# Partial sums of the second softmax on GpSimd in three batches, and another instruction order

## The chip, the cores and the metric

One core of one Trainium2 chip runs the kernel. The metric is the device time of one execution in microseconds; three runs of the kernel before are shown, and a hardware profile of one execution.

## The reference

There are 8 batches of 8 heads with 576 tokens of 64 features, and 32 packed queries `p` per head. Attention runs twice, and a token-mixing layer follows.

```python
def sm_attn(qq, kk, vv):                    # scale = 1/8
    s = scale * np.matmul(qq, kk.transpose(0, 1, 3, 2))
    s = s - np.max(s, axis=-1, keepdims=True)
    a = np.exp(s)
    a = a / (np.sum(a, axis=-1, keepdims=True) + 1e-09)
    return np.matmul(a, vv)
p_packed = sm_attn(p, k, v)                 # 32 rows per head
x = sm_attn(q, p_packed, p_packed)          # softmax over groups of 32
# x: (8, 576, 512) after the heads are put side by side
wq = x @ w_q;  wk = x @ w_k                 # 512 -> 64
W_tok = 0.125 * np.einsum('bsd,btd->bst', wq, wk)
mixed = np.einsum('bst,btd->bsd', W_tok, x)
out = np.maximum(mixed, 0.0) @ w_out
```

## The kernel before

Everything is written out as named operations, one closure each, and a string `SCHEDULE` says in which order they are issued. An item is `name@batch`, with the engine behind it where there is a choice (`v` VectorE, `s` ScalarE, `g` GpSimd, `p` SyncE), or the PSUM banks (`:31`) and a way to split a matmul into column halves (`c` all halves, `p` part, `f` none). Each engine works through its own queue in this order and waits on semaphores for what it needs. Nothing is reordered later: the string is the schedule.

The work of a batch, with the names that the text uses:

- `LK`, `LQ`, `LV` (line 153) load `k`, `q`, `v` of a batch through GpSimd's queue and cast to bf16 on the way; six buffers each. Batch 0 is loaded in halves (`LQA`, `LVB` and so on; `cA0` to `cB1` cast its `k`).
- `kt0` to `kt2` and `qt0` to `qt2` (line 262) transpose `k` and `q` on TensorE; `ke`, `qe` copy the result out of PSUM (`evict`, lines 141 to 149). For batch 0 the same steps are `kf`, `kfe`, `qf`, `qfe`.
- `s0` (321) computes the scores of the packed queries, `nm0` (335) their negative maximum on VectorE, `ex0`, `ex1` (344) the exponentials with their sums on ScalarE, `rc1` (360) the reciprocals.
- `xt0`, `xt1` (399) transpose the exponentials, `xe` copies them, `pv` (423) multiplies with `v`, `pp0`, `pp1` (439) scale the result, `pt` (453) transposes it, `pte` copies. In batch 0 these are done by halves: `xa`, `xb`, `xea`, `xeb`, `pvA`, `pvB`, `ptA`, `ptB`, `pteA`, `pteB`.
- `e0` (494, 507) computes the scores of the second attention: 128 rows with 36 groups of 32. `mx0` (523) takes the maximum of each group, `sb0` (526) subtracts it, `x0` (533) is the exponential on ScalarE in fp32, `sm0` (537, tile `rs`) sums each group, `rr0` (540) takes the reciprocal, `ml0` to `ml2` (561, tile `a`) multiply on GpSimd. Batch 0 does it in two parts (`mxA`, `mxB`, ...).
- `at`, `ae` transpose the normalised weights; `pq`, `pqe`, `wk`, `wke`, `wkx`, `wq`, `wqe`, `g`, `ge`, `y`, `ye` form the small factors of the mixing layer; `m0`, `m1`, `m2` (697, 719) apply them and `r00` to `r11`, `r2` are the evictions with ReLU.
- `o0` to `o4` (737) multiply with `w_out`, `oe0` to `oe4` evict, and `st0` to `st2` or `sc0` to `sc3` store.

`s0` and `e0` share one PSUM tile of three banks; the other results of TensorE go to five single banks. `wm` are matmuls without use ahead of and between the first steps.

The operation that the changed order begins to use is already defined, from line 549, but no item of the string before names it:

```python
def sm(b):
    src = S_[b].get("e4", S_[b].get("e3", S_[b]["e2"]))
    nc.vector.tensor_reduce(tile("rs", [P, NU, 1], fp32, b)[:, r], src[:, r], axis=AX, op=ADD)
...
def sp1(b):
    e = S_[b]["e2"]
    nc.gpsimd.tensor_tensor(tile("e3", [P, NU, L // 2], fp32, b), e[:, :, 0:L // 2], e[:, :, L // 2:L], op=ADD)
```

`NU` is 36 and `L` is 32, so `sp1` writes 36 groups of 16, and `sm` reads them where they exist.

Of the kernel before, what the change touches and what calls it, by code (L numbers as in the profile page):

```python
# [7 lines left out]


SCHEDULE = """  # L10
    wm@8:4 LP@0 LQA@0 LVA@0 cA0@0s cA1@0v LQB@0 wm@1:4 pc@0v kf1@0:2 LVB@0 tp@0:0 kf0@0:4
# [11 lines left out]
    pt@1:0c xe0@2v pte@1s m1@0:23 xe1@2v e0@1:c r10@0s LK@6 rc1@2 r11@0v kt1@3:4 mx0@1
    kt0@3:0 ke1@3s kt2@3:1 LK@5 ke2@3s pq@1:4 sb0@1 o1@0:3c pqe@1s LQ@4 o2@0:4c ke0@3v x0@1
    oe1@0v s0@3 oe2@0s o0@0:3c sm0@1 qt0@2:4 oe0@0s qt1@2:0 rr0@1 qt2@2:1 qe1@2s nm0@3
    o3@0:3c ml0@1g qe0@2s ml2@1g oe3@0v at0@1:2f ex1@3 ml1@1g pv@2:40 ae0@1v ex0@3 qe2@2v
    LV@4 at1@1:2c pp0@2 xt0@3:1f ae1@1s pp1@2 LQ@5 xt1@3:3f rc1@3 xe0@3v pt@2:0c wk@1:2c
    pte@2s e0@2:f wkx@1 LK@7 wke@1s kt0@4:4 xe1@3s mx0@2 g@1:1c wq@1:0 ge@1s y@1:2 wqe@1s
# [7 lines left out]
    qt2@4:4 pv@4:13 qe2@4s rr0@3 nm0@5 ml0@3g pq@3:4 g@2:0c pqe@3s LQ@7 pp1@4 ge@2s qt1@4:4
    ex1@5 pp0@4 y@2:3 ml1@3g ke1@6v pt@4:1f ye@2s at0@3:0f qe1@4v pte@4s m0@2:32 ex0@5
    ae0@3v ml2@3g m1@2:14 r00@2v LV@6 qt1@5:0 r01@2s e0@4:p qe1@5v LV@7 r10@2s xt1@5:3f
    mx0@4 at1@3:0f xt0@5:1f ae1@3s o1@2:2f xe1@5s sb0@4 qt0@5:0 xe0@5s wq@3:3 oe1@2s o0@2:1c
# [2 lines left out]
    rr0@4 qe2@5s s0@7 pp1@5 ml0@4g pp0@5 oe3@2s y@3:0 xt1@6:2f nm0@7 pt@5:1f xe1@6s ml2@4g
    xt0@6:4f at0@4:3f ml1@4g ye@3s o2@2:2f ae0@4v ex1@7 pte@5v at1@4:0f xe0@6v oe2@2s
    m2@3:1f ae1@4v qt0@6:4 ex0@7 rc1@6 st1@2 pq@4:3 qt2@6:0 qe0@6v qt0@7:2 pqe@4s st1@1
    qe2@6v e0@5:c r2@3s st0@2 qe0@7s wk@4:0f mx0@5 st0@1 xt0@7:4c wke@4s m1@3:23 o4@3:1f
    r11@3s wkx@4 r10@3s sb0@5 g@4:3f pv@6:02 ge@4s oe4@3s xe0@7v qt1@6:1 pp1@6 y@4:4 wq@4:3
    pp0@6 qe1@6s qt2@7:2 ye@4v xt1@7:0c x0@5 qe2@7v pt@6:4c o2@3:1f pte@6v xe1@7v wqe@4s
    sm0@5 o3@3:4f oe2@3s qt1@7:0 oe3@3s e0@6:p rr0@5 qe1@7v ml0@5g st1@3 m0@4:41 rc1@7 mx0@6
    pv@7:23 r01@4s ml2@5g r00@4s m0@3:10 ml1@5g pp1@7 o1@4:4c r01@3s pp0@7 r00@3s sb0@6
    pq@5:0 at0@5:2c pqe@5s at1@5:3c ae0@5s pt@7:1c o0@3:0c ae1@5v x0@6 pte@7v wk@5:2p  # L50
    o1@3:3c wkx@5 oe1@4s sm0@6 wke@5s m1@4:41 oe1@3s e0@7:p r11@4s wq@5:3 rr0@6 oe0@3s mx0@7
    g@5:2c ml0@6g r10@4s o0@4:1c st0@3 ge@5s wqe@5s st2@3 y@5:2 ml2@6g o3@4:0c sb0@7 ml1@6g
    ye@5s oe0@4s pq@6:2 at0@6:3c oe3@4s m2@5:4c pqe@6v st0@4 at1@6:1c x0@7 ae0@6v m0@5:20
    ae1@6v o2@4:3c r00@5v r2@5s sm0@7 wk@6:1p r01@5s o4@5:2c oe2@4s wq@6:0 wke@6v st1@4
    oe4@5s wkx@6 m1@5:43 rr0@7 g@6:1c st2@5 r10@5s r11@5v o0@5:2c ml2@7g ge@6s wqe@6v ml1@7g
    o3@5:1c oe0@5v ml0@7g at1@7:0c y@6:4 pq@7:3 o2@5:2c ye@6s pqe@7v oe3@5s ae1@7v at0@7:4c
    m0@6:31 ae0@7s o1@5:0c r00@6v oe2@5s r01@6v wk@7:3p st1@5 oe1@5s m1@6:24 wkx@7 o0@6:1c
    r10@6v st0@5 wke@7s r11@6s g@7:3c oe0@6s o1@6:2c ge@7v y@7:3 wq@7:0 oe1@6s o2@6:1c ye@7s
# [770 lines left out]
```

## Time and profile before

| what | value |
|---|---|
| median of 3 runs (121.89 to 122.12) | 122.09 us |
| profiled execution | 122.1 us |
| its span, first to last instruction | 120.3 us |
| granted TensorE clock | 0.996 |
| TensorE busy | 109.1 us (91%), 2121 matmuls |
| VectorE busy | 99.4 us (83%), 176 instructions |
| ScalarE busy | 86.8 us (72%), 169 instructions |
| GpSimd busy | 44.7 us (37%), 70 instructions |
| loads through GpSimd's queue | 14.49 MB, 72.2% of 16 DMA engines' span |

Busy times are unions over the span, and the engines overlap. The difference between the profiled execution and its span, 1.8 us, lies before the first and behind the last instruction. The end of a matmul is modelled, so that a TensorE shown as busy can still be one that streams with small gaps. Two instructions of VectorE or ScalarE in a row overlap by some 0.08 to 0.1 us in the timeline, so that the step from start to start is a little shorter than the duration in the row.

### The profile page before, as it was taken

The numbers are of one execution on the slowest core, as the hardware profiler recorded it, in microseconds if no ns is written. First come the engines' busy times: TensorE is split into PE (matmuls) and PEld (weight loads), VectorE is DVE, ScalarE is ACT, GpSimd is POOL, SyncE is SP. The second block draws the span as 40 slices with busy tenths as digits, with TensorE's granted clock in tenths as the row PEclk, the third lists the DMA queues.
The fourth block names the chain that finished last, engine by engine and source line by source line (L and its number), as shares of the span: only waits on it lengthen the run. The fifth ranks groups of instructions, "written<-read, shape, count | busy, mean of one in ns | idle before, by whom it ended". The sixth has DMA issues, their size and how long they took to land.

```text
span 120.3 us, 4812 instructions
## 1 busy us (share of the span) xinstructions
PE 109.1 (91%) x2121; PEld 76.5 (64%) x2121; DVE 99.4 (83%) x176; ACT 86.8 (72%) x169; POOL 44.7 (37%) x70
## 2 busy tenths in 40 slices
PE   5999786588999999999999999999999999999950
...
DVE  3278799968999979999999999989998999566330
ACT  4228634688568869996988999996889995665530
...
GB/s 70 375 165 195 207 208 190 207 208 206 211 205 212 204 209 208 206 208 207 208 226 306 290 209 208 209 255 398 225 180 1 106 335 197 70 230 267 185 291 171
DMA packets 18165, 25.47 MB, mean 212 GB/s; under 512 B 2272, under 2 KB 14816, under 8 KB 18144
## 3 DMA queue, kind: packets, MB, share of 16 engines
q0 software_dynamic: 13952, 14.49, 72.2%
...
q10 hardware_dynamic: 288, 0.39, 0.9%
q8 instruction: 16, 0.26, 0.8%
q14 instruction: 5, 0.04, 0.1%
...
## 4 chain that ended last, share of the span: by engine, by line
PE 70%; DVE 19%; POOL 2%; ACT 2%; issue 2%; POOLq 0%; DVEq 0%
PE o_ps L737 24%; PE tp_h L262 9%; PE warm L787 6%; PE pv L423 4%; PE m_ps L697 4%; PE tp_a L582 3%; DVE rs L537 3%; PE e_ps L507 3%; PE wq_ps L642 3%; PE tp_x L399 2%; POOL a L561 2%; PE s L321 2%; DVE e L526 2%; DVE mx L523 2%; PE wk_ps L619 2%
## 5 line engine op out<-in xcount | busy, mean ns | idle before, releaser
L561 POOL TENSOR_TENSOR a<-e,rr 128x512 bf16<-128x512 f32 (+1 forms) x24 | 19.3, 828 | 50.4 <-DVE rr L540 45.1
L737 PE MATMUL o_ps<-w_out,reluT 128*64 128x512 bf16 (+2 forms) x236 | 32.3, 373 | 0.1
L737 PEld LDWEIGHTS <-reluT 128*64 128x64 bf16 (+1 forms) x236 | 13.8, 108 | 9.6 <-issue 1.0
L143 ACT ACTIVATE o_sb<-o_ps 128x512 f32<-128x512 f32 x25 | 14.9, 602 | 3.7 <-PE o_ps L737 3.2
L143 ACT ACTIVATE kT<-tp_h 128x768 bf16<-128x768 bf16 (+2 forms) x13 | 9.8, 794 | 5.7 <-PE tp_h L262 5.6
L143 ACT ACTIVATE reluT<-m_ps 128x512 bf16<-128x512 f32 x20 | 11.5, 600 | 2.5 <-PE m_ps L697 2.2
L344 ACT ACTIVATE e1T<-s,nmax 128x576 bf16<-128x576 f32 x16 | 11.8, 755 | 0.6 <-DVE nmax L338 0.5
L262 PE MATMUL tp_h<-ident,q_sb 128*64 128x128 bf16 x288 | 11.9, 221 | 0.2 <-ACT pqk L143 0.2
L533 ACT ACTIVATE e<-e 128x1152 f32<-128x1152 f32 (+2 forms) x9 | 9.5, 1059 | 3.3 <-DVE e L526 3.3
L262 PEld LDWEIGHTS <-q_sb 128*64 128x64 bf16 x288 | 9.8, 110 | 2.8 <-issue 1.7
L523 DVE TENSOR_REDUCE mx<-e_ps 128x36 f32<-128x1152 f32 (+2 forms) x9 | 10.9, 1208 | 0.7 <-PE e_ps L507 0.4
L262 PE MATMUL tp_h<-ident,k_sb 128*64 128x128 bf16 x288 | 11.3, 226 | 0.0
L526 DVE TENSOR_TENSOR e<-e_ps,mx 128x1152 f32<-128x1152 f32 (+2 forms) x9 | 11.0, 1221 | 0.3
L537 DVE TENSOR_REDUCE rs<-e 128x36 f32<-128x1152 f32 (+2 forms) x9 | 10.9, 1211 | 0.2 <-ACT e L533 0.2
L262 PEld LDWEIGHTS <-k_sb 128*64 128x64 bf16 x288 | 9.7, 114 | 1.0 <-issue 0.2
L787 PE MATMUL warm<-ident 128*64 128x512 bf16 x44 | 8.4, 488 | 1.5 <-POOL ident masks.py:199 1.4
L335 DVE TENSOR_REDUCE nmax<-s 128x2 f32<-128x1152 f32 x7 | 9.3, 1327 | 0.0
L145 DVE TENSOR_SCALAR reluT<-m_ps 128x512 bf16<-128x512 f32 x12 | 8.1, 679 | 1.3 <-PE m_ps L697 1.3
L149 DVE COPY qT<-tp_h 128x768 bf16<-128x768 bf16 (+2 forms) x16 | 8.4, 533 | 0.8 <-PE tp_h L262 0.4
L423 PE MATMUL pv<-v_sb,e 64*128 64x256 bf16 x126 | 8.1, 270 | 0.0
L582 PE MATMUL tp_a<-ident,a 128*64 128x128 bf16 (+1 forms) x113 | 6.4, 221 | 1.7 <-POOL a L561 1.7
L143 ACT ACTIVATE qT<-tp_h 128x768 bf16<-128x768 bf16 (+1 forms) x9 | 7.1, 798 | 0.9 <-PE tp_h L262 0.7
...
## 6 DMA issues: line engine op xcount, KB each, us to landing
...
k_sb<-in_k_dram POOLq DMA_DIRECT2D x7, 576.0 KB, 14.3
q_sb<-in_q_dram POOLq DMA_DIRECT2D x7, 576.0 KB, 18.3
v_sb<-in_v_dram POOLq DMA_DIRECT2D x7, 576.0 KB, 16.4
k_f<-in_k_dram SPq DMA_DIRECT2D x2, 576.0 KB, 4.3
...
```

What stands on the lines that cost most here:

```text
L143: nc.scalar.activation(dst, src, func, scale=scale)
L262: nc.tensor.transpose(dst[64 * g2:64 * g2 + 64], src[:, g2], ident)
L344: nc.scalar.activation(tile("e1T", [P, NJ, 2, 64], bf16, b)[:, :, h2], S_[b]["s1"][0][h2].rearrange("r (j s) -> r j s", j=NJ), EXP, bias=S ...
L423: nc.tensor.matmul(ps[h2], S_[b]["e1"][r, j, :], S_[b]["v_sb"][r, :, j, :].rearrange("s (g gp) d -> s gp g d", gp=2), start=(j == 0), stop ...
L523: nc.vector.tensor_reduce(tile("mx", [P, NU, 1], fp32, b)[:, r], S_[b]["e"][:, r], axis=AX, op=MAX)
L526: nc.vector.tensor_tensor(tile("e2", [P, NU, L], fp32, b)[:, r], S_[b]["e"][:, r], S_[b]["mx"][:, r].to_broadcast((P, nu, L)), op=SUB,)
L533: nc.scalar.activation(e, e, EXP, scale=scale)
L537: nc.vector.tensor_reduce(tile("rs", [P, NU, 1], fp32, b)[:, r], src[:, r], axis=AX, op=ADD)
L561: (nc.gpsimd if on == "g" else nc.vector).tensor_tensor(tile("a2", [P, NU, L], bf16, b)[:, r], S_[b]["e2"][:, r], S_[b]["rr"][:, r].to_bro ...
L582: nc.tensor.transpose(tp[r, k - k0], a2(b, k % 4 if k < 8 else 4, k // 4)[:, r], ident)
L737: nc.tensor.matmul(ps[r], src[:, i, o:o + P][:, r], w_out[:, i, cols], start=(i == 0), stop=(i == 3),)
L787: nc.tensor.matmul(ps[r], ident[:, r], moving, start=True, stop=True)
```

## The change

Only `SCHEDULE` changes. Three items are new, `sp1@2`, `sp1@3` and `sp1@4`: in these batches GpSimd adds the first and the second 16 of each group of 32 exponentials, and `sm0` sums 16 per group. Batches 0, 1, 5, 6, 7 sum 32 as before. All other items are the same operations in another order: 38 evictions go from `v` to `s` and 34 from `s` to `v`, eight projections (five of them of batch 7) go from `c` to `f` and one from `f` to `c`, banks are assigned anew, and the 22 pairs of `wm` are spread differently. The string has one line more, so lines of the changed kernel are higher by one. The lines with batch 0's softmax, with the new items and with the end:

```diff
 SCHEDULE = """
...
-    wm@1:3 xa0@0:3 nmB@0 xa1@0:0 xea0@0s qf0@0:2 rcA@0 xea1@0v ex1@0 qf1@0:1 cw1@0 qfe0@0v
-    pvA@0:0 qfe1@0s xb0@0:4 pp0@0 xb1@0:2 xeb0@0s LQ@1 rcB@0 xeb1@0v ptA@0:1f qf3@0:3
-    pteA@0s qfe3@0v e0A@0 wm@4:1 mxA@0 sbA@0 pvB@0:0 LV@1 qf2@0:2 xA@0 pp1@0 qfe2@0v
+    xa1@0:2 rcA@0 sB@0 xea0@0v xea1@0s qf1@0:3 nmB@0 cw2@0 pvA@0:4 qfe1@0s qf0@0:0 ex1@0
+    pp0@0 wm@1:1 qfe0@0v ptA@0:1c LQ@1 rcB@0 xb1@0:3 pteA@0v xb0@0:0 e0A@0 xeb0@0v wm@2:4
+    xeb1@0v mxA@0 qf2@0:2 qfe2@0s pvB@0:4 sbA@0 pp1@0 qf3@0:2 xA@0 qfe3@0v ptB@0:3f smA@0
...
-    kt1@2:0 ke2@2s ml1@0g pq@0:2 ke1@2v pqe@0s wo0@0 ex1@1 at1@0:1c ae1@0v wo1@0 ex0@1
-    ke0@2v wq@0:1 LQ@2 wk@0:2p wqe@0s LV@2 s0@2 wkx@0 qt0@1:4 wke@0s LK@4 nm0@2 xt0@1:3f
+    kt1@2:3 ml1@0g pq@0:0 ex0@1 pqe@0v wo1@0 at1@0:1c ke1@2v ex1@1 wo0@0 ae1@0v ke2@2v
+    wk@0:3p LQ@2 wq@0:0 wkx@0 LV@2 s0@2 rc1@1 wke@0v wqe@0s xt1@1:4f LK@4 nm0@2 xt0@1:2f
...
-    r01@1v s0@4 x0@2 pp0@3 o0@1:3c pp1@3 nm0@4 r2@1s qt2@3:2 pq@2:0 qt0@3:4 qe2@3s o1@1:1c
-    qe0@3v pqe@2s sm0@2 oe0@1s o4@1:2c oe1@1s qt1@3:0 ex1@4 pt@3:3c qe1@3v kt2@6:1 ex0@4
+    o0@1:4c nm0@4 x0@2 qt1@3:1 o1@1:3c oe0@1s pp1@3 sp1@2 ex1@4 qe1@3v qt0@3:0 pp0@3 qt2@3:1
+    oe1@1s LQ@5 sm0@2 pq@2:4 o4@1:2c qe0@3s qe2@3v pqe@2s pt@3:3c ex0@4 kt2@6:1 pte@3v
...
-    ke2@5s o2@1:4f ae1@2v ae0@2s xt1@4:0f rc1@4 oe4@1s oe2@1v kt0@5:3 x0@3 wk@2:1p ke0@5v
-    st2@1 qt0@4:4 xe1@4v s0@5 wkx@2 qe0@4s st0@0 sm0@3 wq@2:0 wke@2s kt1@6:2 st1@0 wqe@2s
+    ke2@5s o2@1:4c ae0@2v ae1@2s rc1@4 oe4@1v kt0@5:1 x0@3 wk@2:0c ke0@5v st2@1 xt1@4:3f
+    wke@2v s0@5 oe2@1s wkx@2 sp1@3 qt0@4:1 xe1@4s st0@0 nm0@5 wq@2:2 qe0@4s st1@0 g@2:0c
+    qt2@4:4 wqe@2s sm0@3 pv@4:31 qe2@4s ge@2v rr0@3 ex0@5 kt1@6:2 pp1@4 ml0@3g pq@3:0 pp0@4
...
-    rc1@5 r11@2v wqe@3s qe0@5v wk@3:2p x0@4 s0@6 wkx@3 wke@3v kt0@7:4 oe0@2s nm0@6 kt2@7:3
-    kt1@7:0 ke0@7s qt2@5:2 g@3:1f ke2@7s ke1@7v o3@2:4f sm0@4 ex1@6 pv@5:30 ex0@6 ge@3v
+    oe1@2s xe0@5v wk@3:4p x0@4 o0@2:3c wkx@3 nm0@6 qt0@5:1 wke@3s kt0@7:2 sp1@4 oe0@2s
+    kt1@7:4 ke0@7s kt2@7:0 ke1@7v g@3:3f LV@6 ex1@6 sm0@4 o3@2:2f LV@7 ex0@6 ge@3v rr0@4
+    pv@5:43 qe0@5v ke2@7s ml1@4g oe3@2s s0@7 pp1@5 ml2@4g pp0@5 ml0@4g y@3:0 qt2@5:1 nm0@7
...
-    r00@7v r01@7s st1@6 o3@7:1c oe4@7s o1@7:2c st2@7 oe3@7v o0@7:0c oe1@7s sc3@7p o2b@7:3c
-    sc1@7p oe0@7s o2a@7:2c oe2b@7v sc0@7s oe2a@7v sc2b@7s sc2a@7p
+    o3@6:3f r00@7v r01@7s m2@7:1f oe3@6s o0@7:0f r2@7v st1@6 o2a@7:3f oe0@7s o3@7:1f oe2a@7s
+    sc0@7p sc2a@7s o4@7:2f oe3@7s o1@7:4f sc3@7p oe4@7s o2b@7:1f st2@7 oe1@7s oe2b@7v sc1@7s
+    sc2b@7p
 """
```

More of the change, by code (lines that the diff above doesn't have):

```diff
@@ L10 @@
 SCHEDULE = """
-    wm@8:4 LP@0 LQA@0 LVA@0 cA0@0s cA1@0v LQB@0 wm@1:4 pc@0v kf1@0:2 LVB@0 tp@0:0 kf0@0:4
-    lp@0v LK@1 wm@3:3 kfe0@0s kfe1@0v wm@2:3 cB1@0v LK@2 cB0@0v sA@0 wm@1:3 cw3@0 nmA@0
-    kf3@0:1 kf2@0:3 kfe3@0s cw0@0 tr@0:42 kfe2@0v ex0@0 wm@2:3 lq1@0v lq0@0s sB@0 cw2@0
-    wm@1:3 xa0@0:3 nmB@0 xa1@0:0 xea0@0s qf0@0:2 rcA@0 xea1@0v ex1@0 qf1@0:1 cw1@0 qfe0@0v
-    pvA@0:0 qfe1@0s xb0@0:4 pp0@0 xb1@0:2 xeb0@0s LQ@1 rcB@0 xeb1@0v ptA@0:1f qf3@0:3
-    pteA@0s qfe3@0v e0A@0 wm@4:1 mxA@0 sbA@0 pvB@0:0 LV@1 qf2@0:2 xA@0 pp1@0 qfe2@0v
@@ L17 @@
-    ptB@0:4c smA@0 pteB@0s e0B@0 rrA@0 mxB@0 ml0@0g kt2@1:3 kt1@1:1 sbB@0 ke2@1s kt0@1:0
-    LK@3 at0@0:4c ke0@1v xB@0 ke1@1v ae0@0s smB@0 s0@1 kt0@2:4 rrB@0 nm0@1 kt2@2:1 ml2@0g
-    kt1@2:0 ke2@2s ml1@0g pq@0:2 ke1@2v pqe@0s wo0@0 ex1@1 at1@0:1c ae1@0v wo1@0 ex0@1
-    ke0@2v wq@0:1 LQ@2 wk@0:2p wqe@0s LV@2 s0@2 wkx@0 qt0@1:4 wke@0s LK@4 nm0@2 xt0@1:3f
-    g@0:1f LV@3 qt1@1:0 ge@0s xe0@1s y@0:2 qe1@1v xt1@1:1c ye@0s rc1@1 xe1@1v ex0@2 m0@0:30
-    pv@1:21 r00@0v LQ@3 ex1@2 qe0@1v r01@0s qt2@1:3 pp1@1 xt0@2:4c pp0@1 xt1@2:1c qe2@1v
@@ L23 @@
[L23 to L28, printed above, removed]
@@ L29 @@
-    kt1@4:3 ye@1v kt2@4:1 ke0@4v ke1@4s pv@3:02 sb0@2 LV@5 ke2@4s m0@1:43 m2@1:1c r00@1s
-    r01@1v s0@4 x0@2 pp0@3 o0@1:3c pp1@3 nm0@4 r2@1s qt2@3:2 pq@2:0 qt0@3:4 qe2@3s o1@1:1c
-    qe0@3v pqe@2s sm0@2 oe0@1s o4@1:2c oe1@1s qt1@3:0 ex1@4 pt@3:3c qe1@3v kt2@6:1 ex0@4
-    pte@3v m1@1:40 rr0@2 kt0@6:3 r10@1s r11@1v e0@3:c ml1@2g ke2@6s ke0@6v o3@1:0f mx0@3
-    ml2@2g ml0@2g xt0@4:3f oe3@1s kt1@5:4 xe0@4v kt2@5:0 LQ@6 ke1@5s sb0@3 at1@2:3f at0@2:1f
-    ke2@5s o2@1:4f ae1@2v ae0@2s xt1@4:0f rc1@4 oe4@1s oe2@1v kt0@5:3 x0@3 wk@2:1p ke0@5v
@@ L35 @@
-    st2@1 qt0@4:4 xe1@4v s0@5 wkx@2 qe0@4s st0@0 sm0@3 wq@2:0 wke@2s kt1@6:2 st1@0 wqe@2s
[L36 to L39, printed above, removed]
-    rc1@5 r11@2v wqe@3s qe0@5v wk@3:2p x0@4 s0@6 wkx@3 wke@3v kt0@7:4 oe0@2s nm0@6 kt2@7:3
@@ L41 @@
-    kt1@7:0 ke0@7s qt2@5:2 g@3:1f ke2@7s ke1@7v o3@2:4f sm0@4 ex1@6 pv@5:30 ex0@6 ge@3v
[L42 to L58, printed above, removed]
@@ L59 @@
-    wqe@7v st0@6 m2@7:4c oe2@6v m1@7:02 o3@6:3c r11@7s r2@7v r10@7s m0@7:42 oe3@6s o4@7:0c
-    r00@7v r01@7s st1@6 o3@7:1c oe4@7s o1@7:2c st2@7 oe3@7v o0@7:0c oe1@7s sc3@7p o2b@7:3c
-    sc1@7p oe0@7s o2a@7:2c oe2b@7v sc0@7s oe2a@7v sc2b@7s sc2a@7p
+    wm@8:2 LP@0 LQA@0 LVA@0 cA0@0v LQB@0 wm@2:2 pc@0s cA1@0s wm@1:0 LVB@0 kf0@0:0 tp@0:4
+    LK@1 kf1@0:1 kfe0@0s lp@0v wm@1:2 wm@3:2 kfe1@0v LK@2 cB1@0s cB0@0v sA@0 cw3@0 kf3@0:2
+    nmA@0 kf2@0:0 tr@0:31 cw1@0 kfe3@0v ex0@0 kfe2@0v wm@4:4 lq1@0v lq0@0s cw0@0 xa0@0:0
@@ new lines @@
+    xa1@0:2 rcA@0 sB@0 xea0@0v xea1@0s qf1@0:3 nmB@0 cw2@0 pvA@0:4 qfe1@0s qf0@0:0 ex1@0
+    pp0@0 wm@1:1 qfe0@0v ptA@0:1c LQ@1 rcB@0 xb1@0:3 pteA@0v xb0@0:0 e0A@0 xeb0@0v wm@2:4
+    xeb1@0v mxA@0 qf2@0:2 qfe2@0s pvB@0:4 sbA@0 pp1@0 qf3@0:2 xA@0 qfe3@0v ptB@0:3f smA@0
+    pteB@0s e0B@0 rrA@0 mxB@0 ml0@0g kt2@1:3 kt1@1:4 sbB@0 ke2@1s kt0@1:1 LV@1 at0@0:2c
+    ke1@1v xB@0 LK@3 ke0@1v ae0@0s smB@0 s0@1 kt0@2:0 rrB@0 nm0@1 kt2@2:4 ke0@2s ml2@0g
+    kt1@2:3 ml1@0g pq@0:0 ex0@1 pqe@0v wo1@0 at1@0:1c ke1@2v ex1@1 wo0@0 ae1@0v ke2@2v
@@ new lines @@
+    wk@0:3p LQ@2 wq@0:0 wkx@0 LV@2 s0@2 rc1@1 wke@0v wqe@0s xt1@1:4f LK@4 nm0@2 xt0@1:2f
+    xe1@1s g@0:1f LV@3 qt0@1:3 ge@0s xe0@1s y@0:1 qe0@1v qt1@1:4 qt2@1:0 ye@0s qe1@1v ex1@2
+    m0@0:31 pv@1:42 r01@0v ex0@2 LQ@3 r00@0s xt0@2:1c pp0@1 qe2@1s pp1@1 m1@0:43 pt@1:2c
+    r11@0v pte@1s xe0@2s e0@1:c LK@6 r10@0s pq@1:2 mx0@1 kt1@3:3 pqe@1s kt2@3:1 LK@5
+    xt1@2:4c ke2@3s kt0@3:0 sb0@1 ke1@3s o2@0:2c o1@0:1c ke0@3v x0@1 oe2@0v s0@3 xe1@2s
+    o0@0:2c sm0@1 oe1@0s qt1@2:4 oe0@0s qt0@2:0 rr0@1 o3@0:3c nm0@3 qe0@2s ml0@1g qt2@2:1
@@ new lines @@
+    qe1@2s ml1@1g rc1@2 oe3@0v at0@1:2c ex0@3 pv@2:04 ae0@1v ex1@3 ml2@1g qe2@2v LQ@4
+    at1@1:3c pp1@2 xt1@3:2f ae1@1s pp0@2 LV@4 xt0@3:1f xe1@3v pt@2:4c wk@1:2c pte@2s xe0@3s
+    e0@2:f wke@1v wkx@1 wq@1:0 mx0@2 g@1:2c kt0@4:4 ge@1s wqe@1s y@1:2 kt1@4:3 rc1@3 ye@1v
+    kt2@4:1 ke1@4s ke0@4v pv@3:20 sb0@2 ke2@4s m0@1:43 m2@1:1c r00@1s r01@1v s0@4 r2@1s
+    o0@1:4c nm0@4 x0@2 qt1@3:1 o1@1:3c oe0@1s pp1@3 sp1@2 ex1@4 qe1@3v qt0@3:0 pp0@3 qt2@3:1
+    oe1@1s LQ@5 sm0@2 pq@2:4 o4@1:2c qe0@3s qe2@3v pqe@2s pt@3:3c ex0@4 kt2@6:1 pte@3v
@@ new lines @@
+    m1@1:04 rr0@2 kt0@6:3 r10@1v r11@1s ml2@2g e0@3:c ke2@6s ml0@2g o3@1:0f mx0@3 ke0@6s
+    ml1@2g xt0@4:1f oe3@1s kt1@5:4 xe0@4v LK@7 kt2@5:0 ke1@5s sb0@3 at0@2:1f LV@5 at1@2:3f
+    ke2@5s o2@1:4c ae0@2v ae1@2s rc1@4 oe4@1v kt0@5:1 x0@3 wk@2:0c ke0@5v st2@1 xt1@4:3f
+    wke@2v s0@5 oe2@1s wkx@2 sp1@3 qt0@4:1 xe1@4s st0@0 nm0@5 wq@2:2 qe0@4s st1@0 g@2:0c
+    qt2@4:4 wqe@2s sm0@3 pv@4:31 qe2@4s ge@2v rr0@3 ex0@5 kt1@6:2 pp1@4 ml0@3g pq@3:0 pp0@4
+    y@2:4 qt1@4:1 pqe@3s ye@2v ex1@5 pt@4:0f qe1@4v LQ@6 at0@3:4f pte@4v m0@2:31 ml1@3g
```

19 lines of the change are left out of this document (added).

## The prediction

> **What bounds the kernel now.** I began with the busy tenths and the DMA row of the page. TensorE and VectorE alternate between 9 and less until the twelfth slice, then both read 9 almost throughout; the loads move a steady 205 to 210 GB/s up to slice 20.
>
> ```profile
> PE   5999786588999999999999999999999999999950
> DVE  3278799968999979999999999989998999566330
> ACT  4228634688568869996988999996889995665530
> GB/s 70 375 165 195 207 208 190 207 208 206 211 205 212 204 209 208 206 208 207 208 226 306 290 209 208 209 255 398 225 180 1 106 335 197 70 230 267 185 291 171
> ```
>
> Then the busy times by stage, cut where TensorE starts `pv` of batches 2, 5 and 7 (40.3, 72.75, 87.4 us) and where it stops (116.1).
>
> ```profile
> 0.00:40.30 40.30, 33.73 (x662) 24.26 (x662) 32.32 (x63) 23.89 (x48) 23.23 (x44) 1.00 1.16 204
> 40.30:72.75 32.45, 32.19 (x688) 24.35 (x688) 31.03 (x52) 28.87 (x56) 11.85 (x15) 1.00 1.19 226
> 72.75:87.40 14.65, 14.58 (x288) 10.49 (x289) 13.86 (x28) 12.27 (x26) 2.70 (x4) 1.00 1.03 258
> 87.40:116.10 28.70, 28.63 (x492) 17.38 (x486) 21.75 (x36) 21.75 (x42) 6.94 (x9) 1.00 0.49 179
> ```
>
> The third busy column is VectorE: 31.03 of 32.45 in the second stage, so VectorE and TensorE are both full there. The last stage is TensorE's alone (28.63 of 28.70; VectorE 21.75). The chain of waits leaves TensorE once in the middle, at 57.8 us, for VectorE's queue:
>
> ```profile
> 59.41 0.33 DVE wkx L632
> 59.74 1.27 DVE rs L537
> 61.04 0.38 DVE rr L540
> 61.41 1.21 DVE nmax L335
> 62.63 0.79 DVE pp L439 x2
> ```
>
> So a shorter `rs` (op `sm0`) lies on the path. Last, when the loads land. The issue of `LV@5` starts at 44.16 and takes 27.1 us, so it lands at 71.3; `pv@5`, which needs it, starts at 72.75. Likewise `LQ@7` lands at 77.0 (use 77.7), `LV@6` at 79.8 (81.5), `LV@7` at 84.2 (87.4). TensorE never waits for a load, but here it runs only 0.7 to 3.2 us behind them.
>
> ```profile
> v_sb<-in_v_dram POOLq DMA_DIRECT2D x1, 576.0 KB, 27.1
> ```
> ```profile
> 72.75 1.16 PE L423 MATMUL pv<-v_sb,e 64*128 64x256 bf16 x18
> ```
>
> The prices come from the groups by shape:
>
> ```profile
> L561 POOL TENSOR_TENSOR a<-e,rr 128x512 bf16<-128x512 f32 x16 | 16.7, 1044 | 44.6 <-DVE rr L540 39.3 <-ACT qT L143 5.3
> L561 POOL TENSOR_TENSOR a<-e,rr 128x128 bf16<-128x128 f32 x8 | 3.2, 395 | 5.8 <-DVE rr L540 5.8
> L537 DVE TENSOR_REDUCE rs<-e 128x36 f32<-128x1152 f32 x7 | 9.4, 1344 | 0.2 <-ACT e L533 0.2
> L537 DVE TENSOR_REDUCE rs<-e 128x20 f32<-128x640 f32 x1 | 0.8, 809 | 0.0
> L537 DVE TENSOR_REDUCE rs<-e 128x16 f32<-128x512 f32 x1 | 0.7, 685 | 0.0
> ```
>
> **The change part by part.** *Sums on VectorE.* From 685 ns at 512 and 809 at 640 elements, 576 take 0.75 us in place of 1.34: 3 x 0.6 = -1.8 us, all in the two middle stages.
>
> *Adds on GpSimd.* From 395 ns at 128 and 1044 at 512, a multiply costs 1.69 ns an element; 576 would be 1.15 us. Bounds: 1.04 (the 512 row) and, since an fp32 result and two full inputs are not in the trace, twice 1.04, 2.1. I take 1.15, the nearest kind. Three cost 3.5 us on an engine busy for 11.85 of 32.45 us, hence nothing by themselves. The new wait is `x0` to `sp1` to `sm0`. Between `x0@2` and `sm0@2` VectorE's order holds `pp1@3`, `qe1@3`, `pp0@3` (1.25 us), so the cover is bare; ahead of `sm0@3` and `sm0@4` lie some 2 us (`nm0` among them). At 2.1 us the three waits come to about 2 us. Queued behind `sm0` are `rr0` and the evictions `pte@3`, `ge@2`, `pp@4`, `pp@5`, for which `e0` of the next batch waits. On GpSimd, `LQ@5` stands behind `sp1@2`, `LK@7` and `LV@5` behind the three multiplies of batch 2, `LV@6` and `LV@7` behind `sp1@4`. The loads keep their order, and their transfers, one after another at 2.8 us each, start at 58.3, 61.1, 65, 77 and 80 us; the issues move to about 50, 54, 55, 69 and 70, still 6 us ahead: nothing.
>
> *Evictions that change engine.* 38 go from VectorE to ScalarE and 34 the other way. With the steps from start to start in the timeline (VectorE: a 768-column copy 0.47, a 512 one from fp32 PSUM 0.60, 256 columns 0.34; ScalarE 0.70, 0.48, 0.28) VectorE loses 17.2 and gains 14.6 us, -2.6; ScalarE gains 4.8. With the sums, VectorE's steps up to `pv@2`, from there to `pv@5`, to `pv@7` and to the end were 29.6, 31.1, 14.1, 20.0 and become 28.5, 29.0, 14.0, 19.0; ScalarE's were 21.0, 27.2, 11.3, 19.6 and become 23.2, 28.0, 12.3, 20.4. TensorE has the same columns and the same 22 warm-up pairs.
>
> *First stage.* VectorE's -1.1, and more: it idles 0.45 before `ae1@0` and 0.70 before `wkx@0`. There the new order has `pqe@0`, `ke1@2` and `ke2@2`, and `wk@0` (0.45) before `wq@0` (0.62), so `wkx@0` comes sooner. Walking the queues with these steps from the landing of k: `nmB` stays at 11.5, but one eviction of `xea` is now ScalarE's and the other lies ahead of `nmB`, so `pp0@0` starts at 12.25, not 13.37; `mxA` at 14.25, not 15.21; `mx0@1` at 31.65, not 33.09; `pv@2` at 38.7, not 40.3. Between -1.1 (the work alone) and -2.2 (work and both idle times) I take the walk's -1.6. `LV@2` landed at 38.1, so it fits.
>
> *Middle.* VectorE's -2.1 to `pv@5` would bring that to 72.75 - 1.6 - 2.1 = 69.0; the walk, with its waits, gives 70.1. But `LV@5` lands at 71.3: the bytes ahead of it in the queues are the same (three stores, `st2@1`, `st0@0`, `st1@0`, stay before it). TensorE waits there until 71.35: the gain is cut to -1.4, with 1.2 to 2.3 us of spare that hide other losses up to that point. From `pv@5` to `pv@7` VectorE's work is unchanged. The stores of batch 2 come 1.1 us sooner and will share the engines with `LV@6`; `LV@7` took 4.4 us with them and 2.8 without, so up to 0.6 is lost, I take 0.2.
>
> *End.* From `pv@7` TensorE is the limit with the same work. Eight projections go undivided: 28 matmuls of 128 columns took 7.0 us, 1.0 per projection, and 192 of 64 took 24.3, 1.01 per projection: nothing. The last evictions and stores swap names and keep their number after the last matmul: 4.2 us as before, give or take 0.1.
>
> Sum: -1.4 + 0.2 = -1.2. The profiled execution took 122.1 us (span 120.3, 1.8 around it), as much as the median of 122.09; so **120.9**. This case reaches from 120.2 (nothing lost to the stores, 0.1 at the end, and 0.4 if part of the three stores, for which `LV@5` took 6.3 us after `LK@7` instead of 2.8, slips behind it) to 121.5 (adds at 2.1 us, 0.6 lost to the stores).
>
> [...] GpSimd ran its 24 multiplies beside a full VectorE at 389 to 395 and 1038 to 1060 ns, and the copies of VectorE beside those of batch 2 (53.5 to 55.9 us) took 0.54 and 0.48, as elsewhere. [...]
>
> **The rivals.** *Blocked VectorE, 0.04.* [...]
>
> *Loads do not limit, 0.07.* If `LV@5` to `LV@7` land sooner, VectorE's -3.4 up to `pv@7` comes through in part, about -2.5: 119.6. Against it: the loads run without a gap to 84 us.
>
> *Nothing left, 0.13.* In the second stage VectorE and ScalarE now stand at 29.0 and 28.0 beside TensorE's 29; three equally full in-order queues wait for each other more. If that eats 1.2 us beyond the spare, it is 122.1.
>
> *ScalarE late, 0.26.* It takes 4.8 us more. In the second stage it is busy for 28.87 and idle for 3.58. If those idle times are waits that stay, and the 0.9 us is added, the stage is 33.3; if the first stage also gains nothing, as ScalarE has 2.2 us more there, `pv@5` starts at 40.3 + 33.3 = 73.6 instead of 72.75, and the end is 123.0. It decides once the walk's 70.1 slips by over 2.65 us. For it: a ScalarE step that is late holds a PSUM bank and so TensorE. Against: its longest waits in that stage are 0.6 to 0.8 us.
>
> **How the numbers follow.** The forecast has 0.50. About 0.2% (0.24 us) is what a measurement can tell. Faster: 0.50 + 0.07 and 0.05 from "nothing left" and "blocked", 0.62; same: 0.09 from those two; slower: 0.26 + 0.03 = 0.29. The range goes from the low end of the forecast's case to the middle of "ScalarE late" and leaves out the 0.07 below and half of the 0.26 above: 120.2 to 123.0.
>
> **What would show it.** Right: three 576-element adds of about 1.15 us; `rs` at 0.75 three times; `mxA` near 14.3 and `pv@2` near 38.7; TensorE waiting for `LV@5` until about 71.3; `pv@7` to the last matmul 28.5. Wrong: `pv@5` after 72.5 with ScalarE's evictions ending TensorE's waits; adds over 2 us; `LV@5` landing elsewhere; TensorE idle after 88 us.

## The result and the profile after

The changed kernel takes 123.21 us (median of 11 runs, 122.47 to 124.09), the kernel before beside it 121.98 us (11 runs, 121.4 to 122.32): a ratio of 1.0102, with a 95% interval of 1.0074 to 1.013. It is slower, and lies above the range of the prediction too. The profiled execution took 122.64 us (span 120.9), so it lies at the low end of its runs.

The rows of the page of the changed kernel that answer to those of before:

```profile
PE   5999975699899999999989999999999999999900
...
DVE  3198899998699799979999988899999995776010
ACT  4267256769789869989989998999799995556610
...
GB/s 72 366 183 200 208 208 188 207 208 206 209 206 211 205 209 208 207 209 207 208 263 321 239 208 207 208 297 395 148 0 5 240 353 190 87 264 221 350 249 59
```

VectorE now reads 7 and 8 in more slices of the middle, ScalarE 9 more often, and TensorE reads 0 in the last two slices, where before it read 5 in the second last. Then the busy times by stage, cut where the changed kernel starts `pv` of batches 2, 5 and 7 and where TensorE stops (length, TensorE, its weight loads, VectorE, ScalarE, GpSimd):

```profile
0.00:39.26 39.26, 33.27 (x664) 23.22 (x664) 31.69 (x61) 26.09 (x50) 22.36 (x42) 1.00 1.15 206
39.26:71.66 32.40, 31.74 (x677) 23.71 (x677) 29.98 (x54) 29.42 (x55) 16.40 (x20) 1.00 1.19 226
71.66:86.44 14.78, 14.48 (x296) 10.86 (x299) 13.35 (x25) 13.68 (x27) 3.65 (x5) 1.00 1.07 264
86.44:115.04 28.60, 28.39 (x450) 16.71 (x446) 20.62 (x34) 22.05 (x43) 6.42 (x9) 1.00 0.49 183
```

Beside the stages of before (40.30, 32.45, 14.65, 28.70) the first is 1.04 us shorter, and the others are 0.05 shorter, 0.13 longer and 0.10 shorter: TensorE stops at 115.04 instead of 116.07. But the span then goes on for 5.8 us (120.86 - 115.04) where it was 4.3 (120.33 - 116.07). So in this execution the body won 1.0 us and the end lost 1.6.

What happens in the end shows in the DMA view of the last microseconds, in slices of 0.1 us from 117 to 121, first of the kernel before and then of the changed one:

```profile
GB/s 471 389 348 369 328 389 410 430 369 328 328 328 369 328 348 328 338 175 21 0 0 0 0 0 0 0 0 0 0 0 0 0 0 0 0 0 0 0 0 0
```
```profile
GB/s 123 164 164 287 451 348 389 348 379 389 338 389 226 164 0 0 0 20 10 10 10 10 10 10 0 0 0 0 0 0 0 0 0 0 0 0 0 0 0 0
...
q14 instruction: 1, 0.01, 0.5%
```

Before, the stores stop all at once at 118.8. After, fifteen of the sixteen engines have sent their data by 118.4; for 0.3 us no packet starts at all, and then a single engine trickles 1 KB packets, one in 0.1 us (10 GB/s), until 119.4. Queue 14, which carries instructions, has one packet in this window, of 8 KB, from 118.40 to 118.71. The last store (issued at 115.89) reports done from fifteen engines within 2.89 us and from the sixteenth after 3.95. The issues on SyncE's queue (start, length, line, tiles, how many), first of the kernel before and then of the changed one, show what is new: the store of `sc3`, both of `st2` and `sc2b` stand one behind the other:

```profile
113.27 1.15 SPq L754 DMA_DIRECT2D out_dram<-ox  x2
114.66 2.45 SPq L764 DMA_DIRECT2D out_dram<-o_sb  x3
```
```profile
112.24 2.27 SPq L765 DMA_DIRECT2D out_dram<-o_sb  x2
114.61 1.19 SPq L755 DMA_DIRECT2D out_dram<-ox  x2
115.89 0.57 SPq L765 DMA_DIRECT2D out_dram<-o_sb  x1
```

The last begins 0.85 us behind the last matmul; before, it was 0.49, and ScalarE's queue sent another at the same time. The groups by shape, for the new and the changed steps:

```profile
L553 POOL TENSOR_TENSOR e<-e 128x576 f32<-128x576 f32 x3 | 4.3, 1422 | 12.6 <-ACT e L534 12.6
...
L538 DVE TENSOR_REDUCE rs<-e 128x36 f32<-128x576 f32 x3 | 2.2, 747 | 0.1
```

### The profile page after: what moved, and what is told of

It is laid out like the page before. It is cut to its first block, busy times and chain, and to the rows that moved or that the text cites. A ratio compares the mean times of both kernels' runs of the same rounds, so it can differ in the third digit from the quotient of the medians.

```text
span 120.9 us, 4729 instructions
## 1 busy us (share of the span) xinstructions
PE 107.9 (89%) x2073; PEld 74.5 (62%) x2081; DVE 96.1 (79%) x172; ACT 91.4 (76%) x173; POOL 48.8 (40%) x73
## 4 chain that ended last, share of the span: by engine, by line
PE 52%; DVE 16%; DMA 9%; issue 8%; ACT 5%; POOL 5%; SPq 1%; POOLq 0%; ACTq 0%
PE o_ps L738 16%; PE tp_h L263 7%; DMA out_dram<-o_sb 5%; DMA k_f<-in_k_dram 4%; PE m_ps L698 4%; PE pv L424 4%; PE tp_a L583 3%; DVE rs L538 3%; PE s L322 3%; PE e_ps L508 2%; DVE e L527 2%; DVE mx L524 2%; PE wq_ps L643 2%; PE tp_x L400 2%; POOL a L562 2%
## 5 line engine op out<-in xcount | busy, mean ns | idle before, releaser
L738 PEld LDWEIGHTS <-reluT 128*64 128x64 bf16 (+1 forms) x208 | 13.1, 107 | 9.7 <-issue 0.8
L144 ACT ACTIVATE o_sb<-o_ps 128x512 f32<-128x512 f32 (+1 forms) x25 | 14.7, 595 | 2.3 <-PE o_ps L738 1.6
L144 ACT ACTIVATE reluT<-m_ps 128x512 bf16<-128x512 f32 x22 | 12.8, 604 | 2.1 <-PE m_ps L698 1.9
L144 ACT ACTIVATE qT<-tp_h 128x768 bf16<-128x768 bf16 (+2 forms) x14 | 11.0, 793 | 2.5 <-PE tp_h L263 2.4
L144 ACT ACTIVATE kT<-tp_h 128x768 bf16<-128x768 bf16 (+1 forms) x13 | 10.0, 802 | 2.7 <-PE tp_h L263 2.5
L538 DVE TENSOR_REDUCE rs<-e 128x36 f32<-128x1152 f32 (+3 forms) x9 | 9.1, 1013 | 0.3 <-ACT e L534 0.2
L553 POOL TENSOR_TENSOR e<-e 128x576 f32<-128x576 f32 x3 | 4.3, 1422 | 12.6 <-ACT e L534 12.6
L788 PE MATMUL warm<-ident 128*64 128x512 bf16 x44 | 7.4, 453 | 1.5 <-POOL ident masks.py:199 1.4
L150 DVE COPY o_sb<-o_ps 128x512 f32<-128x512 f32 (+1 forms) x8 | 5.2, 653 | 4.0 <-DMA out_dram<-o_sb 3.7
L146 DVE TENSOR_SCALAR reluT<-m_ps 128x512 bf16<-128x512 f32 x10 | 6.9, 687 | 1.9 <-PE m_ps L698 1.7
## 6 DMA issues: line engine op xcount, KB each, us to landing
q_sb<-in_q_dram POOLq DMA_DIRECT2D x7, 576.0 KB, 11.4
```

What stands on the lines that cost most here:

```text
L144: nc.scalar.activation(dst, src, func, scale=scale)
L738: nc.tensor.matmul(ps[r], src[:, i, o:o + P][:, r], w_out[:, i, cols], start=(i == 0), stop=(i == 3),)
L788: nc.tensor.matmul(ps[r], ident[:, r], moving, start=True, stop=True)
```

## Experiments

Ratios are those to the kernel before on the same chip, with 95% intervals; "the gap" is the time from the last matmul to the last store's landing in the profiled execution (3.2 us before, 4.8 after).

### Which part of the order: e1 to e4

e1 and e2 cut both orders at `pv@7` and cross them; one `ml` and `st1@3` change sides with the cut, so that each item is issued once. e3 takes the three adds out of the new order, e4 puts them into the old one:

```diff
 e3, new order
-pp1@3 sp1@2 ex1@4
+pp1@3 ex1@4
-wkx@2 sp1@3 qt0@4:1
+wkx@2 qt0@4:1
-kt0@7:2 sp1@4 oe0@2s
+kt0@7:2 oe0@2s
 e4, old order
-x0@2 pp0@3
+x0@2 sp1@2 pp0@3
-x0@3 wk@2:1p
+x0@3 sp1@3 wk@2:1p
-sm0@3 wq@2:0 ... rr0@3 nm0@5
+wq@2:0 ... nm0@5 sm0@3 rr0@3
-x0@4 s0@6
+x0@4 sp1@4 s0@6
```

> The new order up to pv@7, with its three adds, and the old order behind it. Theory A (the new body is ahead by 1.0 us, the new order of the end loses it and 1.6 us more after the last matmul): the body's gain is kept, 0.9 to 1.2 us faster than the kernel before, 120.8 to 121.1, with the last landing 3.2 us behind the last matmul. Rival B (the loss lies in the body, and the profiled execution of the changed kernel, at 122.6 against a median of 123.2, is a lucky one): 122.8 to 123.2, slower than before. Rival C (the end is lost whatever its order, because it starts sooner and meets the same stores): same as before, 122.0.

Measured: 122.02 us, 1.0019 (0.9996 to 1.0041). This is rival C's number: the loss of the end is gone, and so is the gain of the body that theory A kept.

> The old order up to pv@7, without adds, and the new order behind it. Theory A: the last matmul stays at 116.1 us of the span and the last landing comes 4.2 to 4.9 us behind it instead of 3.2, so 1.1 to 2.2 us slower than before, 123.1 to 124.2. Rival B: as before, 122.0 within 0.3.

Measured: 123.0 us, 1.0107 (1.0076 to 1.0138), at the low end of theory A.

> The new order without its three adds; VectorE sums 32 in every batch. If the shorter sums brought the body's lead of 1.0 us: 1 to 1.8 us slower than the changed kernel (pv@7 at 87.4 to 88.2 in the profile instead of 86.4). If the lead is the order's alone, made in the first 39 us: pv@7 stays within 0.3 of 86.4 and the time within 0.3% of the changed kernel's 123.2.

Measured: 123.35 us, 1.0125 (1.0096 to 1.0154). The time is within 0.3% of the changed kernel's, as the second theory said, but `pv@7` starts at 88.30 us, as the first one said. Both can be so because the end of e3 is 1.0 us shorter (a gap of 3.8 us instead of 4.8).

> The old order with the three adds put behind x0 of batches 2 to 4, and sm0 and rr0 of batch 3 moved behind nm0 of batch 5; nothing else. If VectorE is the limit of the middle stage: 1.0 to 1.5 us faster than before, 120.5 to 121.0, pv@5 at 71.4 (where LV@5 lands) instead of 72.75. If TensorE or the loads are the limit there: same as before within 0.3, pv@5 within 0.3 of 72.75. If the wait for the add (1.42 us measured in the changed kernel, 0.27 over my price) takes it back: 122.3 to 123.

Measured: 121.6 us, 0.998 (0.9959 to 1.0001).

With the old end the loss is gone (e1), and the new end behind the old body brings all of it (e2). The adds cost nothing; in the old order they are worth 0.2% by the medians, and the interval reaches 1.000. In e2 the last issue comes 1.30 us behind the last matmul, where it was 0.49, because four transfers of 0.6 us each stand in SyncE's queue. These four alone would make the new end itself the whole loss; e9 below shows that behind its own body it is not.

### What in the end: e5 to e8

```diff
 e5: halves of o2@7 in tiles of their own
+        if half is not None:
+            evict(on, tile(f"oh{half}", [P, D // 2], fp32, b), ps)
+            return
 e6
-o2a@7:3f oe0@7s o3@7:1f oe2a@7s sc0@7p sc2a@7s o4@7:2f oe3@7s o1@7:4f sc3@7p oe4@7s o2b@7:1f st2@7 ...
+o4@7:2f oe0@7s o2a@7:3f oe4@7s sc0@7p st2@7 o3@7:1f oe2a@7s sc2a@7s o1@7:4f oe3@7s sc3@7p o2b@7:1f ...
 e7
-r00@5v st1@3 r2@5s                 and  oe2@6s st2@5 o3@6:3f
+mx0@6 st1@3 pv@7:23                and  g@6:3c st2@5 pq@7:2
 e8
-o2@6:4f o3@6:3f m2@7:1f o0@7:0f o2a@7:3f o3@7:1f o4@7:2f o1@7:4f o2b@7:1f
+o2@6:4c o3@6:3c m2@7:1c o0@7:0c o2a@7:3c o3@7:1c o4@7:2c o1@7:4c o2b@7:1c
```

> The new order, but the two column halves of o2@7 are evicted into two tiles of their own, so that oe2b no longer waits for the store of oe2a to land. The new order stands at 1.010 of the kernel before. False-wait theory: that wait (3.69 us of VectorE's idle time in the trace) delays the last store, and 0.4 to 0.8 us come back: 1.003 to 1.007. Issue theory (SyncE's queue hands out its stores one after another at some 0.62 us each, and oe2b is ready before sc2b's turn comes): the wait of oe2b on VectorE is then on TensorE alone, and the time stays at 1.009 to 1.011.

Measured: 122.31 us, 1.0027 (1.0004 to 1.005).

> The new order, but o4@7, oe4@7 and the two transfers of st2@7 stand ahead of o2a, so that behind sc2a only sc3 and sc2b are left in SyncE's queue. Same operations. Issue theory: the last issue comes some 0.5 us behind the last matmul as in the kernel before, instead of 0.85 to 1.3, and the gap from the last matmul to the last landing falls from 3.8 to 4.8 us to 3.0 to 3.4: a gain of 0.5 to 1.2 us, 1.000 to 1.006. Bunching theory (too many stores are left for the last 20 us): nothing, 1.009 to 1.011, as the same bytes leave in the same time.

Measured: 122.55 us, 1.0046 (1.0022 to 1.0069). The last issue does come 0.54 us behind the last matmul, but the last store takes 3.22 us, the last 0.9 of them on one engine.

> The new order, but st1@3 and st2@5 stand where the old order has them, some 10 us sooner. The end of the order, sc3, st2@7, sc2b in SyncE's queue, is as changed. Bunching theory: the stores of the last 15 us land 0.4 to 1 us sooner, 1.002 to 1.007. Issue theory: no change, 1.009 to 1.011.

Measured: 121.84 us, 0.9992 (0.9972 to 1.0013).

> The new order with the eight undivided projections of batches 6 and 7 (and m2@7) divided into column halves as before. If undivided projections cost at the end (an eviction that cannot begin before the whole projection is done, 9 times up to 0.1 us on TensorE): up to 0.5 us faster, 1.006. Issue theory: no change, 1.009 to 1.011. The prediction's price for this step was nothing.

Measured: 123.07 us, 1.0089 (1.0061 to 1.0117): undividing the projections cost nothing. (Of the eight, `o2@4` stays undivided here.)

The wait for a store's landing (e5) and the late stores (e7) each seemed to explain most of the loss, which cannot both be so. Their traces have something else in common: the instruction fetch comes after the end, at 120.8 and 120.6 us, while in e6 and e8 it is at 118.1 and 118.6, among the last stores. And both edits take two instructions off VectorE: counted with its waits, its trace has 192 records instead of 194.

### The fetch alone: e9, e10, e12, e15, e16

These add instructions that do nothing for the output, ahead of all work, where VectorE and ScalarE wait for the first load (in the changed kernel VectorE is idle from 2.2 to 4.6 us, ScalarE from 2.0 to 4.8):

```diff
     nc.vector.memset(tile("pp", [P, 2, 256], bf16, 0), 0.0)
+    pad = sbp.tile([P, 4], bf16, name="pad")
+    for i in range(4):                             # e10: range(1); e18: range(10)
+        nc.vector.memset(pad[:, i:i + 1], 0.0)     # e12: evict("s", pad[:, i:i + 1], ident[:, i:i + 1])
```

e9 and e12 do this to the changed kernel, e10 and e16 to e1, e15 to e6.

> The new order as it is, and four memsets of one column each on VectorE ahead of everything, while it waits for its first load (it is idle until 4.7 us). They do no work for the output. In the traces so far, the runs of the new order that lose most (1.009 to 1.010) have an 8 KB instruction fetch on one DMA engine at 118.4 to 118.6 us, in the middle of the last stores, and on that engine the last store lands 1.1 us behind the other fifteen; the runs that came out near 1.000 to 1.003 have two instructions less on VectorE (192 instead of 194 records), and there the fetch comes after the end (120.6 to 120.8). Fetch theory: VectorE's place in its code sets the fetch, four more instructions bring it to 112 to 116 us, the last store lands 2.8 to 3.0 us after its issue instead of 3.95, and the time falls by 0.6 to 1.1 us, to 1.001 to 1.005. Store theory (late stores and the wait of oe2b are the cause themselves): no change, 1.009 to 1.011.

Measured: 121.91 us, 1.0015 (0.9992 to 1.0038). The last fetch of the run is at 111.7 us. In the same DMA view, the trickle is gone, and so is queue 14:

```profile
GB/s 184 184 143 103 205 246 369 471 430 369 328 389 359 358 287 92 10 0 0 0 0 0 0 0 0 0 0 0 0 0 0 0 0 0 0 0 0 0 0 0
```

> The new order and four copies of one column on ScalarE ahead of everything (no work for the output). If VectorE's code sets the late fetch, it stays at 118 to 119 us and the time at 1.008 to 1.011; if ScalarE's does, the fetch moves ahead and the time falls to 1.001 to 1.005.

Measured: 123.45 us, 1.011 (1.0075 to 1.0145), beside the same runs of the kernel before as e9. The fetch stays among the last stores, at 119.15 us, and one engine trickles:

```profile
GB/s 184 184 205 328 123 205 82 184 143 123 266 369 369 348 399 430 348 338 348 338 174 103 0 0 20 10 0 10 10 10 20 0 0 0 0 0 0 0 0 0
...
q14 instruction: 1, 0.01, 0.5%
```

> The converse: the new order with the old end (1.002, its fetch at 120.5 us, after the end) and one memset of one column on VectorE ahead of everything, which makes 194 records as in the changed kernel. Fetch theory: the fetch moves into the last stores (117.5 to 119 us) and the time rises by 0.5 to 1.0 us, to 1.006 to 1.010. Store theory: one idle instruction more at the start does nothing, 1.000 to 1.004.

Measured: 122.63 us, 1.0057 (1.0034 to 1.008). One memset of one column, put ahead of everything, moves the fetch from 120.5 to 118.6 us, and the kernel, which stood at 1.0019 without it (e1), loses.

> The new order with st2@7 ahead of o2a (1.005 alone, with the fetch at 118.1 us in its last stores) and the four idle memsets on VectorE. Fetch theory: the fetch comes at 111 to 113 us, the last store lands 2.3 us after its issue, not 3.2, and the time falls by 0.6 to 1.0 us: 0.996 to 1.000. If what is left of its loss is the late stores st1@3 and st2@5, it stays at 1.002 to 1.005.

Measured: 121.93 us, 0.9994 (0.9971 to 1.0018).

> The new order up to pv@7 with the old end, and four idle memsets on VectorE, so that the fetch comes before the last stores (113 to 116 us) and not at 120.5 (1.002 without them, 1.006 with one). This is what the new order's body is worth without its end: pv@5 and pv@7 start 0.5 to 0.7 us sooner in the runs of the new order than of the old, and the gap behind the last matmul is 3.1 us in both: 0.994 to 0.998. If the body brings nothing: 1.000 to 1.002.

Measured: 122.02 us, 1.0004 (0.9983 to 1.0025). The body of the new order is worth nothing by the medians.

### What limits the middle: e13, e14

The projections of batch 1 contract two of four blocks, in the old order and in the old order with adds:

```diff
-        for i in range(4):
+        ni = 2 if b == 1 else 4
+        for i in range(ni):
```

> The old order without adds; the five projections of batch 1 (48 to 58 us) contract only two of their four blocks, which takes some 2.2 us of matmuls out of the stage from pv@3 (45.98) to pv@4 (60.85 us), and nothing from VectorE (rows of batch 1 are wrong in the output). The stage takes 14.9 us as it is. VectorE theory (the prediction's reading: VectorE's queue is full and sets this stage's end): under 0.6 us shorter, 14.3 or more. TensorE theory (TensorE's own matmuls are the limit, and what VectorE gains is idle time): 1.5 us or more shorter, 13.4 or less.

> The same two blocks left out, and the three adds on GpSimd in the old order (0.998 without the cut). The adds alone changed the stage from pv@3 to pv@4 from 14.87 to 14.88 us. TensorE theory: as long as without the adds, within 0.3 us. Both-full theory (each engine alone would hold the stage): with both relieved, 0.6 us or more shorter than with the cut alone. In the time, whatever is won here is cut by the landings of v of batches 5 to 7 (71.3, 79.8, 84.2), so that both kernels end 0 to 1.2 us below the kernel before.

Measured: 0.9975 (0.995 to 1.0) and 0.9974 (0.9951 to 0.9996). The stage from `pv@3` to `pv@4` (length, TensorE, weight loads, VectorE, ScalarE, GpSimd), in the order before, e4, e13, e14:

```profile
45.98:60.85 14.87, 14.87 (x296) 11.33 (x293) 14.60 (x23) 13.73 (x24) 3.16 (x4) 1.00 1.21 208
```
```profile
45.75:60.63 14.88, 14.88 (x298) 11.34 (x294) 13.90 (x23) 13.75 (x24) 5.92 (x6) 1.00 1.21 208
```
```profile
46.25:60.60 14.35, 13.36 (x277) 10.27 (x276) 14.35 (x23) 13.87 (x24) 3.16 (x4) 1.00 1.21 208
```
```profile
45.76:60.12 14.36, 13.28 (x279) 10.21 (x277) 13.93 (x23) 13.88 (x24) 5.99 (x6) 1.00 1.21 208
```

As it is, the stage lasts as long as TensorE is busy in it, 14.87 of 14.87: taking 0.7 us from VectorE (14.60 to 13.90) moves nothing, against the VectorE theory. Taking 1.5 us from TensorE instead moves only 0.5, which is the VectorE theory's number for e13, and then VectorE is full, 14.35 of 14.35. With both taken away, the stage stays at 14.36, as the TensorE theory said, though TensorE, VectorE and ScalarE are each 0.4 to 1.1 us short of full. So neither theory fits all three kernels: as the stage stands TensorE is the limit, with VectorE half a microsecond behind it. What holds e14 at 14.36 stays open.

### Putting the parts together: e11, e17, e18

e11 joins the edits of e6 and e7. e17 takes the new order up to `s0@1` and the order of e4 behind it; e18 adds ten idle memsets to e17.

> The new order with st1@3 and st2@5 early (0.999 alone) and the end with st2@7 ahead of o2a (1.005 alone). VectorE has as many instructions as with the early stores alone, so the fetch theory has the fetch after the end; and the last issue comes 0.5 us after the last matmul instead of 0.8. Both theories: a gap of 3.1 to 3.4 us from the last matmul to the last landing, and 0.994 to 0.999, the fastest so far.

Measured: 121.52 us, 0.9977 (0.9949 to 1.0006), with a gap of 2.9 us.

> What the parts point to: the new order up to s0@1 (batch 0's softmax), then the old order with the three adds, and the old end. In the profiles the first pvA starts at 11.7 us on average with the new start and at 12.45 with the old; from there to pv@7 the old order with adds takes 74.7 us, the new one 75.2; from pv@7 to the last matmul the old end takes 28.7 behind the old body. If these parts add up: 0.6 to 0.8 us below the old order with adds (0.998), 0.992 to 0.996. If the lead of the start is lost again, as in the new order: 0.997 to 1.000. VectorE has as many instructions as in the runs whose fetch came after the end, which may cost 0.2 us behind the last store.

Measured: 122.41 us, 1.005 (1.0031 to 1.0068). VectorE has 194 records here too, and the fetch came at 118.05 us, not after the end as I had counted.

> The same with ten idle memsets on VectorE at the start, which should bring the fetch to 106 to 112 us, ahead of the last stores. Fetch theory: the last store lands 2.5 to 2.6 us after its issue and nothing is added behind it, 0 to 0.3 us below the kernel without the memsets. If the memsets themselves delay the start, it is slower than that by their 0.6 us.

Measured: 121.52 us, 0.9978 (0.9955 to 1.0001). The same DMA view of e17 and then of e18:

```profile
GB/s 246 348 389 410 389 348 369 318 328 348 379 318 328 358 287 103 0 10 10 20 21 31 20 10 0 0 0 0 0 0 0 0 0 0 0 0 0 0 0 0
...
q14 instruction: 1, 0.01, 0.5%
```
```profile
GB/s 451 307 328 338 358 328 338 358 358 174 21 0 0 0 0 0 0 0 0 0 0 0 0 0 0 0 0 0 0 0 0 0 0 0 0 0 0 0 0 0
```

Ten memsets that do nothing save 0.7%. Of the kernels that leave nothing out, e4, e11 and e18 are the fastest, some 0.2% below the kernel before, and the interval of each still reaches 1.000 or beyond.

### All of it in one table

| kernel | VectorE's records | last fetch, us | last store to land, from its issue, us | ratio |
|---|---|---|---|---|
| changed | 194 | 118.4 | 3.95 | 1.0102 |
| e12, four copies on ScalarE | 194 | 119.2 | 3.97 | 1.011 |
| e8, divided | 194 | 118.6 | 3.97 | 1.0089 |
| e10, old end, one memset | 194 | 118.6 | 3.35 | 1.0057 |
| e17, new start | 194 | 118.1 | 3.38 | 1.005 |
| e6, `st2` first | 194 | 118.1 | 3.22 | 1.0046 |
| e1, old end | 193 | 120.5 | 2.55 | 1.0019 |
| e5, halves apart | 192 | 120.8 | 2.84 | 1.0027 |
| e7, early stores | 192 | 120.6 | 2.92 | 0.9992 |
| e11, e6 with e7 | 192 | 120.4 | 2.31 | 0.9977 |
| e9, four memsets | 198 | 111.7 | 2.92 | 1.0015 |
| e15, e6 with four | 198 | 112.1 | 2.57 | 0.9994 |
| e16, e1 with four | 197 | 115.0 | 2.72 | 1.0004 |
| e18, e17 with ten | 204 | 110.9 | 2.55 | 0.9978 |

Among the kernels with parts of the new order, e2 and e3 are the two that lose a full per cent without such a fetch: e2 by its late issues (a gap of 4.0 us) and by 0.4 us from `pv@7` to the last matmul, e3 in its middle (`pv@2` to `pv@5` 33.06 us instead of 32.40, `pv@5` to `pv@7` 15.26 instead of 14.78). Why the same end costs more behind the old body (e2) than behind its own (e9, whose last issue is 0.83 us behind the last matmul) was not followed further.

## Why the prediction was wrong

*The end, "4.2 us as before, give or take 0.1": the step that failed.* From the last matmul the span went on for 5.8 us instead of 4.3. Of the 1.6 us more, 0.4 is the last issue (four transfers in a row in SyncE's queue), and 1.06 is the sixteenth engine of the last store, which is late where a fetch falls among the last stores. I had compared names and numbers of stores and matmuls, and no view of the kernel before shows a fetch in the last stores, as its own came at 115.3 us. That the late sixteenth engine comes and goes with the fetch is shown by e9 against the changed kernel (the store that lands last takes 2.92 us from its issue instead of 3.95), by e16 against e10 (2.72 and 3.35), by e15 against e6 (2.57 and 3.22) and by e18 against e17 (2.55 and 3.38), where nothing differs but idle memsets; that the fetch follows the number of VectorE's instructions and not of ScalarE's, by e12 (119.15 us with four copies on ScalarE, 118.40 without). That the body as such loses nothing is shown by e16.

*The first stage, -1.6.* In the profiled pair the walk was close: `pp0@0` at 12.26 (said 12.25), `mxA` at 14.43 (14.25), `mx0@1` at 31.91 (31.65), `pv@2` at 39.26 (38.7). But all of it is there at the first `pvA` (12.58 before, 11.46 after), and from there to `pv@2` the old order takes 27.75 us and the new one 27.8 (28.2 at most, in e11). And that start scatters: it lies at 11.4 to 12.45 us in the 15 profiled kernels with the new start, 11.74 on average, and at 12.1 to 12.85 in the five with the old one, 12.45 on average. So some 0.7 us is what the start brings, and the pair shows 1.1. That `pv@5` came at 71.66, near the 71.35 that the forecast's parts give, is therefore luck: the lead was all there at `pvA`, and neither the gain in the middle nor the wait for `LV@5` took place.

*The middle, -2.1 cut to -1.4.* The sums came as said (`rs` at 747 ns three times, 1.8 us less), but VectorE's busy time from `pv@2` to `pv@5` fell by half of the 2.1 that was said, from 31.03 to 29.98, and the stage went from 32.45 to 32.40 us. The cap at `LV@5` never came into play: it landed at 70.9 and `pv@5` started at 71.66, right behind a projection. The error was to take VectorE's busy time for elapsed time where the same row had TensorE at 32.19 of 32.45 (the rival "nothing left" even counts it at 29, which no row shows). One of two full engines was relieved. e4 shows that this alone moves nothing, and e13 that relieving the other one does, though by only 0.5 us. The chain of before, which left TensorE for VectorE at 57.8 us, showed where the two meet, not which of them to relieve.

*The adds.* 1.42 us each, where 1.15 was taken; inside the bounds of 1.04 to 2.1. The cover was as bare as said: `sp1` now stands in the chain ahead of `rs`.

```profile
48.66 1.44 POOL e L553
50.12 0.75 DVE rs L538
```

It costs next to nothing there: the stage from `pv@3` to `pv@4`, with two of the adds, takes 14.99 us instead of 14.87. In the new order the adds are worth much more than in the old: without them (e3) it is 1.0125, with them and a harmless fetch (e9) 1.0015.

*From `pv@5` on.* 14.78 us instead of 14.65 to `pv@7` (+0.13, said +0.2), 28.60 instead of 28.70 to the last matmul (said: the same work). The undivided projections cost nothing, as e8 confirms for all but `o2@4`.

*The rivals.* "Nothing left" (122.1) has the body's number, though its mechanism, queues that wait for each other more, was not shown: without the fetch, the new order stands at 1.0015 (e9), and with the old end at 1.0004 (e16). What the start leads by is lost in small parts behind it: on average `pv@7` starts at 86.84 us in the twelve profiled kernels with the whole new body and the adds, and at 87.09 in the three with the old body uncut. "ScalarE late" had a time near the measured one, 123.0, but not its mechanism: it put `pv@5` at 73.6, and it came at 71.66. "Blocked VectorE" had 0.04, but no run shows an add that holds up VectorE: beside the three adds, VectorE's 768-column copies took 0.55 and 0.56 us (0.55 on average before), its `pp` steps 0.47 and 0.48 (0.48), its reductions `nmax` 1.35 and 1.36 (1.33). No rival had the end. Two readings are a little off and change nothing: in slices 5 to 20 the loads move 190 to 212 GB/s, and the multiplies took up to 400 ns where the prediction says 395.
